# Q and K of a block's first 14 tokens, projected in eight pieces between the early steps

## Chip, cores and metric

One core of one Trainium2 chip runs the whole program in one launch. The metric is device time in microseconds; lower is better. All matrix work is bf16 with fp32 accumulation.

## The reference

Two layers share one set of weights. Each is an attention over segments with a memory that is handed from segment to segment, followed by a gated feed-forward block:

```python
def attention(x, mem0, Wq, Wk, Wv, Wo):         # x: 2048 x 512 after layernorm; 32 heads of 128
    mem = mem0                                  # 8 x 512
    for s in range(64):                         # segments of 32 tokens
        h = concat(mem, x[32*s : 32*s + 32])    # 40 x 512
        q, k, v = h @ Wq, h @ Wk, h @ Wv        # 32 heads each
        p = softmax(mask(q @ k.T / sqrt(128)))
        o = (p @ v) @ Wo                        # 40 x 512
        mem = o[:8]                             # the next segment needs it
        out.append(o[8:])

x = x + attention(layernorm(x));  x = x + (sigmoid(n @ w_gate) * (n @ w_up)) @ w_down   # n = layernorm(x)
x = x + attention(layernorm(x));  x = x + (sigmoid(n @ w_gate) * (n @ w_up)) @ w_down
```

The loop over segments is a recurrence through `mem`. The 32 tokens of a segment, though, are known as soon as the layer's input is, so Q and K of those columns can be projected at any earlier time.

## The kernel before

**Steps.** Work goes in 70 steps. Step t handles segment t of layer 1 and, since layer 2 runs `LAG` = 6 segments behind, segment t-6 of layer 2 in the same instructions. In steps 0 to 5 only layer 1 is there (40 columns: 32 tokens and 8 of memory); in steps 6 to 63 both are (80 columns). A tile `hT` of a step holds the transposed columns in the order tokens of layer 1, memory of layer 1, memory of layer 2, tokens of layer 2. Four segments make a block (`BLK` = 4); after a block's last step `ffn` does its feed-forward work, from weights that are streamed in again each time by POOL's queue.

**A step** (`emit_step`). For groups of heads: `qk` (L874) multiplies Wq and Wk of three heads with the step's columns, eight matmuls of 128 rows a head; ScalarE copies the result from PSUM into `qku`; `sc` (L910) makes the scores; VectorE and ScalarE do the softmax; TensorE transposes the probabilities (L956), multiplies them with V (L982), and ScalarE copies that for `wom` (L1001), the product with Wo, which adds up over all heads in one PSUM bank. At the end VectorE copies the memory columns of that bank into the next step's `hT`, and the next step's `qk` can begin.

**Q and K ahead, as it is.** Steps 0 to 5 (`save`) carry 14 columns more than they need: `early_x` puts the first `NE` = 14 tokens of segment t+6 beside step t's 40 columns, so their `qk` matmuls have 54. The 14 columns of the result are copied into the tile `kx` and written to DRAM (`xq`). Steps 6 to 11 (`load`) read them back into `kx` by two loads on SP's queue (L804), copy them into `qku`, and multiply only the other 66 of 80 columns. From step 12 on `qk` has all 80.

**V ahead.** V of most tokens is projected by blocks (`v_group`, `v_pass`, `v_half`; matmuls of 512 columns at L641 and L679) and parked in DRAM (`scr`); a step reads its rows back into `vsb`. The remaining rows are projected in the step (`strips`, L768). The first 80 us do much of this while the weights arrive: SP's queue loads x, then Wv, Wq, Wk and Wo in parts (L519).

**What sets the order.** All work is first recorded as tasks (`pl.add`) with an engine or a choice of two, what they read and write, and an expected duration. `plan` then takes the order of all tasks, and the choice of engine, from a table written into the kernel (`SEQUENCE`, packed text); every engine issues its tasks in that order. `warm` finds places where TensorE is expected to wait over 250 ns and puts filler there: matmuls of a constant tile `hot` into a bank that is free (L1220), in front of the task that waits.

Buffers that matter here: eight PSUM banks (of kind "v" at most three at a time), three staging tiles `vst` of 512 columns that also serve `v_pass`, one tile `kx`.

Of the kernel before, what the change touches and what calls it, by code (L numbers as in the profile page):

```python
# [53 lines left out]
;BKuiVqE|X01NF@%`%$~C5I~V(&DA-OaXtS+oZAk*3k2dJAGvJ`K4rePyr97!Bi{jAHvv%XkRPRfF1TT>3QycOz)(#e7JiZh6=G4BCJyZTa`JjKaw7+_W?k=$6E})3{EOU@GEuz+<S997ZSBsC!UPa`3e^OcZc13UF_jWS_=U@M@Vu  # L54
)?^Jk+S=(nw>o9DjP1NW3k@!Y_JvoI|uSU^QcNCqKm!gxq=`#yCwshxTDLA)Esn^P=$o2#QhSXJq(Ug3|%_wZHnr}Tl_8Z5$+bO03=t|i9?h)?`DR|SsM+Cg&Q?uJ7Bb&sM`2$8v5VHI4nX@*_zXJ05tlt4G$dGzRdZgTL<-u&a!b=
@yXD+zAM8o)rkKOOOuT%HjZRRL_{T^RPv4*|xcO5RXV=8|vZdOw~vpuIyD3^h_6_(A`=3*UfXk+MN9-~d!d-F_dazit{3lXzFn4BJDju4I$46aE|5_!KMwM-+{4PZ7=vHhEyrb&trStNg=4v!m&cAib3%XKKTArFzcQnDlVtgi=)r8
om6Tqq0hLSc931v$`+{_hxn&#7>e1&Az!rOqqPzot<B=D!hO!SyNy?EltBsrbbJpVxv~mXa;L5b~YBU_f$G4VudeQ*O3(>9AvtDlJl{OKBrhU{?6^(=*-Xgwy%hEA)pX44PC^cU^ZmHZ3MCZ*t+;jvC3A_RS$G(Mj7-m`+=WurRZCy
RW28zY7)FoKbost*~b%bZa@p9jN9cHa0Yt#Fzoq4}Ya6mu*)8mcMdw_TJ}CFun0bZMFoV`@4WV>ZR0&vP9|2gE)7d0;@^3vbJsTS)a>Nn=?8EEV1tyZdHth)Ps%K&0<+YcBg|=mAGw8Z{T$*B$OQXT?`{9_o_=h4Xf@73+l@K@Kme7
rTSsNNj$U9aapJ}H@bt|&}0{(8m6TP_0`)w1k-LLm8QCEkk}#PT!IvUZ6`Xx4Ge@-SbjIku4K}0ZoTQur#5otl1{TM^N@TVrJK05=6dxx6T!)_#&JRPWOW?D8_q?1TFdHI5+%-wf);%E?rF3!zC6aZS^<U)sHFB24*bp$eA;{k#*u^
)yy~3m94a{iSuUi?=4SqpCg0p{$w6;cQ{`lv7cW?N%fW!cuXF?7C*b-`ybmC^kr#Z-J1<heQyb3#2Up@yTPY&0g!9H6G#q^RL%goi?9>D&+~tB;9w*b9FgG^XE9=@znb2^<(RBb%VO6eSCVaTWMr;d7r2Bp7u6%+tb>K}1o1$s{136  # L60
KU8Yq|t?_cZE3@=kH4`QW0A<NzV-JkMZB(}*7%LIjmclfqBq7!$M74E!j!t*BMXqjfU+Q2CzTCdu4Fsl?_uuFc<h~6XInEz1iO2>9s2UTmG>4oe)=lAWxqM$>B0#G?Zu)+Q<t|2J1oFIwFvj;e52}KJI>ZhF1JeKj<C<UFGaLv+^-a
pAwsEME4Iv{n%6vMj{i@)b(^3eOK$-Pg!P~%9_7__A*&GXfos!9O|R`Crii%XP^iyZ;`e$f{i)WZuj46Q$$21D7gIr>`JVAJG6ah(f8_s`Lyq2H9j8exyRpWI(#2{M9LD}qZ7pc4|rdJ_8et4OQ;%}a4H^7OQO#DK&p#!rV8^saoyz
87|7bq9VZKoVb6R9I6kNICzvq9rwU>%jiouIYe%Q<u8s8#_i<uTIoT6)-~}3rs!CZs0JK!SS^PSF>Z|t%dXwaS{CX5r#c9(7FT`{Je^*W6kvuv*lyA%(tm^A|YF1Jln6_Q^?fIOWKsFDd=~{D_7cmM&1XVT4FP?8u74bXi%Xx8Lv_b
2gEgT>83KhZBh-1D5!-Knh%wDJaXAjI$p>F4#VWG`mMKZ##Wu(jLTwC_HL22@uc&Nh7<%C$mv6P@;zUwqMO_#%nq=Ya0oenG9LHcaQA+$IBLHpL_&->{@1>-)FQ3$9J>csOv>QDjyee-((A@%asEwA$#}=Muifq>i~4=p6C%msT14k
_I^w>aA2ocBy$^2F8Uy7K8n$OyPLUE3(;AtnL?z2Q5qgrLT_!w<A|b|DIddq#P>B=-$4c&4#WZEY59`AIIEgUZkBJB`y6Ow-qJw5NN?9gjbrbYKB$qUfhB0fx8yx~ZYieTn78*megD#UaIvxCc$+(}_-GlDTglIzBWa9-xNNX;7w`H
ht&Y@+sLo}%F2fS(sv%ktXl&Sz~K^|?0Skg*JY^ok%+ns~LB%q%5w%x@(ne?a8-_VqYY@+h_M^x^iF$3C^ILRBFeq+%*{z?{q$HnX27bK}z3RQE!6+t`Dig!>vOwXNma_iWBPclA;X08N<QZVz~O<B|B5I9&ZLwCs4@8gc&Y5^z}e0
l(+eqe=rU}UqzX4tyL+JK9*n;h)g)k%h>ZQkfDMqk6rA&--EcT{5ha1wTP$IhTO`oZt4OT9mcfJKv&I}!e!*ao=|OXL+wz5Ufv<uKzvsCT_X{{Ygjboh>5zWCKt3Aw}4nr28wy7D@iwKnOyWg{16OcVpIpzeIE{B`2_hCJN-g3Dv(Y
~1LYUP8yQQZAWqPCcd9+_r#5y^F$mR5RfCfX{<qM3bp*52j@@kGCY;&b&3$2ejznzF1RoFaRo!Se#yU?~e2LZJ<u^O*0;vjlczqF$=x!zRl472-RPEL1k~Al&Uxsd6|49mY{jEw^6wK+=lig6!5kJsDRk67Vh@gy6w4I48-$36E9sf
9Mnbu5I@Xd0=d3-uMUzd1nAo#A8nBnkwbq7qvOO*D#~N%zaB1-or!_ht1&0DlEr^>fYPfAqmv>4_tvFs__7$}vtBrk3MmyvCj`+}>J=4&2Vu{F$}%c#s(<aP26uBGMvP(R{_61{SscPw?48<sKKTo(kR>F&(PzG7sw@Cu#4x~^3FV3
p+RNUftl>~V^~%5LvqgQjtFQu`E^_*s`JkX={RM)F1q1>0xYLnEQ0YZQnxSc{scP+?m|WF3pUBGyYi3+D@p;}<s_#1M=%x5|i}|_*($A|TI@63`)AR|>j+?0vf%CE_nHu0seH~qWD`0;Dt}L0FDzJ+9dVF}|iN}@}4rIqQ=?f+J#qH  # L70
i5)Psi_x}I&HQ15}yl7;&_?*&9REL9(KKGF@`xtjg0WnrDb@X*T$rA2-2H78#ee|+Bn&x8w!q{9!Q+>x9oP{sQt#ekY0>*<jpmFpELF7WCfhqE$;YoSEGk61*EouQjWT9MY?W?pEvesBU{l+XHfx0KDJn*&s!hh|!iR)4a8#AiPmv1
LLvXv$dln`A*56_FAuosO*3x!tHHrtdxis{4pe_VAJv8Xi!}B9_F^{<{YosaIxAXNE#&ART>Y91Gj?n7?E3w%XVP(K%eR1a6eSh{Wc8lrJV2$2^L41fr}A#WZR$HdDxdBmsJI(O-;C)cqJ4j?e;~68CX(PvmlCxQ~8{Ua^Qi9#MB0m
4me2(-p-_#ZawJlsR90iaX|P<JHeB+#|4!P)jGgNt>=}eT;tn-PltAX+v<_!HTy<EI)#DyUxZfF>@9k^l7*^UN7PSMm+?BB_eeP;Vh~2F6bCbx&5c2<9ifiDWs01i2==!t};cEkd8K9Do}9%z*w+_Jb6a`<{<<h+e9|klTz3$R0n4m
HexQ=jm2_pHC06xDlLAcW5xKl-i9IgE2nhjw=jDVm!N@O0^;M*&L5@!Zm{&u_`2$p1Doa0NYcNaDZ0K86kXk4o5Ij9HH4;*Oj)A*SPCiv|3x%RDy2+?{6$8+$9oS;L3o4cwdy)Z--^K8D5oD0!6au3D(|Mk%x|49a@v4?00%EdS_q&
&j{SeY$?tyO-u6%Jbo3{b=(C?rZpU}wWC?2bk3;7D+<(#z(N9|oJAeovUsP=nL}sO~o^v2XGhvqSf#3ur`fg;G<oG_aP0TC8pdD;+m`%+W`FZWJr9*WuVJa4#er6%KT86U28;ae(udg<Zv-k-R@h1&QTDMk3o!vuAIJYyIirJf56?d
<-Xfwr#?i-;<41>kClzy8YfqbArK~VEII-;^6si}H~MC`i|M)0X_o~panNVgdjCDwkCp3*0Eg0gz|M*q!i)1?HxY&Jj@+6y`LG!<b{Np=6*5d#2R)#_9uM*sbRO;kOuMMvNP`(8>w6=D+r=rG~ZP&VYBeAGe;^o?2zy6^PBvEx(!6e
z$(yT{5&bxb%&f{awSd#<q~lUusQ{q^|yIgb-Ug+9yV@y0x=_Or8ki1m3q2r<hKx=$#t3s}d`hC~DThmGDnt+xBj*nI=&JmHi_cN#Z0m1L?AI(%ZuK518W$^{<j1hQdwxyz^^@Wafmd{g7v{J;aAzKTQ#GrKLoh+ygzNs5W#FJ=&uG
p}|l^?GB@`bAn6L5+g}$iK$sDY=DwkpX5YHfW{`cKOKQzSD}uDVA4`3`8ma`lL3ieNQ<{{n~T1K%_AgySyZBcLHq*S?lD?%6{JK0KH~F*m?dId|LM4e<lme1S~c!`aE6)-8EjHlvzPipQTO7f;b^<w&X};tDvuBThQQ;Oi=AW;%pU%
e?&D+1t*aW+-$`958=7mXNn=nm{UejM#e0eox1kyG<Jsd2+jt`E=D21V|sx)PXO;yKyRB)U_1Iy&X|Q?Pp}qE2Le}*HPLdcdoslscFd|r(lXC=3Wv=xOK;SBhq1)Bx>Zc<sEr+E&_(wpMhb=w%wR9vA_6DN2k`=9xkchYzG-PXJM(~
?9j$9`lwJK$&tLKsDjugE3x3*yngo^{VFMY=2UObS^~@URJ+vPKvCL7?E6L)NYLXiA-hQ}8<(%MkY0Go3SAgaTrh>jJ`2h!ebyh<YC_fd`17Se@Htq?96`@17%k4Vk?FESFz}b#+^%RkZy8(^tZy%-YWVW$_*;}crd{F@zG_3GGXqw  # L80
G$9YbO)XtO6x_2x4eAxF~Tx;YX>4Ton*ZIXOmY03|wPRSI+sWtMxKXZzfi$noh?)@d+bdqY?!!<znNBuZ7ILccEGMRc)vR0tTD0D;h2X!;aw|#g6`N&SLl9&rZM7F;Twhvx7ptEb(ySd7Yx-Y?k%UDpv#&6StRh28w(Op9D#Z9_ztV
#;M;o3gZY*0*O1@k*QgZ_@VKb%ETY<92_C84tPMi@sI*R@=&Jgl!`Y#|eF7^f%5u^aLe&$CO(^AXGpQKS8P*^^ZvWeEyyp)5C17s=UoD<v6qQSf-jI;;2@L#ook`wTvNlXl_eCj#GL;wwg;kXIkGJ@j6gY^*%KgGSAHmQu@m$_QGS;
@N3g#*u34lpDnGWe!+4XdJ!DEQc_4;RjyH=TRjZA%~v_N$M?|iz3AD-?n_6=^68K#Hzbp9T5+0AjYLm@Bx0P|7#2k2Gh(E2}w-EmJ`4~XsE#(uF>F)zN@78laFrAqHmXlcJ^bm6QLuC)|nG6&+!ZJa$#r|sI+<;fsl(d=%^g%_(iw_
;Z0Bfox{geN`_XCHr3hb@^a^d7xwpE)>1;3;$MT2c?FNa7{tKwf*_l0=23qV_VCkVRH3IXP+@V+>Y?ObbN?HPeP2eU)6U!CshZViN0Jbm0xLN7x`LGhlCKvnCfV@-EV#sWUI^$e$=Zw$+?Nve7RY^fzZoi@4j6>G{e=K{aefg<A@48
lV9kv${kUq+PQtv{yCrJ@?07o}LLmc*1y6X#Q4>ftsa6ksw#MEqE6ikW&hL<`z1;YPhm9((mxU}JF{MRi+`EW)q1dyu2S!ZLrwUX`PfwprgCc5IP2T%IjHEB|t4-lhTd+xP_nckYf<2sG`{vXqb^E)8JP7r5YUMUwcoC`k!Uj(6XCV
20LIxln5Br6W+7(5|H2wHnXwTJS-z6%PGJ(YbY#<!L3m+OpZjVvBv6k{?C9fUtev?!d!Vq_qzc2vj9o!)N*N7s9@=eje51mZhi5x04VDab1XUBgh?ohnGkI>{R+rCttLf+3VSQ)WD`gkqAsStra-r`|dY4V%#AcUMlKYJ_x_~m}mKB
h2m9rH+(T$7op<c;<;og)g_X9bb2=zEGIH|xeA(2Oz+wXT%wrv!60HlrXgBhExJ_s+hYvm{cDXwQ<Q-+2Gv;$;^SlY>ZHn^Q!*#p1d=O6$^$Ve)!Vp#-pIE;$ePR-{svt?B(Zi%!OY9pl<#`p+=kD5@Sb6(bP6@@Va1>1V|>pu!4f;
5%ea8<L^Oyr+svjR@9YJ5Kf<&<>Ar^d7p{N)UuT6skTarIdgc%>!l)%Y~GT5f|-@9G??!<Qa+x9;k0y%G|S9C%VlKV&l_1x){)sH{^$ljb=-yRIkrRQ)UMN0lyj>PGOPSn&e!sjA6jBssbpx{vx>Jqx>o^)s~cov<06%RzAOEKi~<Y
ECQ;@LI7CDY(YDT5hquVL;w~I;_SiK3kuHBwys1Wa<QwQEYISFKbf@ESgj^VG_^?qWyJ)q{_LM0#rZxpQT}|JyTU1Us1tpr))C2dQ*N=(j>U!;KWSu|!g~xms)5xiF#4BSECHxX+CFDyYbrrm(e%4*%BE|T&vEF)6?%EGmyed~A%j7
(Uz<xluJdR+&hXUd|MsBK!7)=Ohihk>MSsY>!bl91J&8t)XCtqA3@O^|M@?;8#L5&lIlmBW+Y<HIabtT_r)T&~LBA&U-p?(#d>yM_tba8Mec%9rKiWC&`CeZ{z%LSnEhyuLJt~7ysp2BR4l9U81tGX@lUbB;YA?Rz;cqlgPI59VGAd  # L90
8*Vf)3*jKqqaKi+mI%BZ-3Ekgl+vDSkZ580)w9*T`y+U2>!oBdMF3e0nfwns6&NbNylou~X_hy2vF+r2Y&OnTT;(t*@wh7~t3bSCsmgmw!erLqjuppC-YP!`&qR79#9NcJonlup=X&QuWM^6DTSZ1J^g4CP&lv&w(dvj8(Nh+|B+TN
N}GzW~xJ4ialVe$%hQqrvsuF-MGB5P;A`h{`HNxqAkn@?!CSlEFe{IKbdbXSaP~!?+l7;-^5xTlsSBtB?1Hcwu?yxzCcPB)x&8pIx)pu468wT}15Mn0Xw&Ts`;ey$?<V7<Gw3A-*xjqOQKBbrvo#0CmNQj~2$gxOO>pv%ICkMNQg$G
={ug{z-8{Jg$ZFCkIhp@H5}gg}U0$sO*zWcq0j4b|Gw~clm9{+IU7){C_y8XDm%NEv8yMkiGd0(z?YH9NgU*;TE#yo;@k5S*=IDt9XhFj@q?bzUN4)$Nh;#LXZ`XsWP)7@K84L1&M*BPx-cY7T{Fr$hTMf+=_4X?8GvmQxMI=Lbsn^
# [1206 lines left out]
```

## Time and profile before

| | us |
|---|---|
| median of 3 runs | 1747.89 |
| lowest, highest | 1745.29, 1750.98 |
| the profiled execution | 1748.87 |
| its span, first to last instruction | 1746.8 |
| TensorE busy in the span | 1733.3 |

The rows of the profile are read so: a group or timeline row names line, engine, operation, the tile written and those read, and shapes; "128x54" after the tiles is the matmul's moving operand, 54 columns. A record of a matmul lasts from its issue to its last result, so records of matmuls that follow each other overlap, and the pace is the distance of their starts. Times are from the start of the span.

### The profile page before, as it was taken

The numbers are of one execution on the slowest core, as the hardware profiler recorded it, in microseconds if no ns is written. First come the engines' busy times: TensorE is split into PE (matmuls) and PEld (weight loads), VectorE is DVE, ScalarE is ACT, GpSimd is POOL, SyncE is SP. The second block draws the span as 40 slices with busy tenths as digits, with TensorE's granted clock in tenths as the row PEclk, the third lists the DMA queues.
The fourth block names the chain that finished last, engine by engine and source line by source line (L and its number), as shares of the span: only waits on it lengthen the run. The fifth ranks groups of instructions, "written<-read, shape, count | busy, mean of one in ns | idle before, by whom it ended". The sixth has DMA issues, their size and how long they took to land.

```text
span 1746.8 us, 91799 instructions
## 1 busy us (share of the span) xinstructions
PE 1733.3 (99%) x39151; PEld 1492.4 (85%) x39151; DVE 1253.9 (72%) x4185; ACT 1143.3 (65%) x3142; POOL 873.5 (50%) x1402
## 2 busy tenths in 40 slices
PE   9999999999999999999999999999999999999998
...
PEclk9999999999999999999999999999999999999999
DMA  9835365655545464646456464646556454555544
GB/s 312 304 103 167 87 177 139 176 144 158 151 132 170 131 185 126 174 125 173 139 152 179 126 177 127 171 124 167 168 134 176 138 152 131 159 150 138 162 135 119
DMA packets 145071, 273.41 MB, mean 157 GB/s; under 512 B 39846, under 2 KB 85930, under 8 KB 144662
## 3 DMA queue, kind: packets, MB, share of 16 engines
...
HBM read 221.78 MB, written 27.07 MB: 142 GB/s over the span
## 4 chain that ended last, share of the span: by engine, by line
PE 94%; DMA 2%; issue 1%; SPq 1%; POOL 1%; ACT 0%; DVE 0%; POOLq 0%
PE bank L874 33%; PE bank L1001 17%; PE bank L1103 11%; PE bank L768 7%; PE bank L641 7%; PE bank L1126 5%; PE bank L910 4%; PE bank L982 4%; PE bank L956 2%; DMA wk_sb<-in_A_Wk_dram 1%; PE bank L601 1%; SPq L1230 1%; PE bank L1071 0%; DMA vsb<-sst 0%; DMA xs<-in_A_x_dram 0%
## 5 line engine op out<-in xcount | busy, mean ns | idle before, releaser
L874 PE MATMUL bank<-hT,wk_sb 128*128 128x80 bf16 (+3 forms) x8960 | 616.9, 198 | 2.3 <-DMA wk_sb<-in_A_Wk_dram 1.8
L874 PE MATMUL bank<-hT,wq_sb 128*128 128x80 bf16 (+3 forms) x8960 | 616.5, 198 | 0.6 <-DVE hT L1014 0.3
L1234 ACT CAST qku<-bank 128x480 bf16<-128x480 f32 (+3 forms) x770 | 383.6, 506 | 208.3 <-PE bank L874 183.7
L874 PEld LDWEIGHTS <-wq_sb 128*128 128x128 bf16 x8960 | 454.0, 99 | 31.6 <-issue 14.3
L874 PEld LDWEIGHTS <-wk_sb 128*128 128x128 bf16 x8960 | 447.5, 99 | 2.9 <-DMA wk_sb<-in_A_Wk_dram 1.9
L1001 PE MATMUL bank<-otsb,wo_sb 128*128 128x80 bf16 (+1 forms) x8960 | 356.2, 198 | 1.9 <-issue 1.9
L924 DVE TENSOR_TENSOR st<-bank,cst 40x240 f32<-40x240 f32 (+3 forms) x768 | 281.2, 368 | 101.2 <-PE bank L910 85.1
L1001 PEld LDWEIGHTS <-wo_sb 128*128 128x128 bf16 x8960 | 333.5, 99 | 12.4 <-issue 2.7
L1230 POOL DMA_DIRECT2D vsb<-sst x360 | 182.2, 510 | 185.9 <-ACT sst L1234 73.7
L1234 ACT CAST otsb<-bank 128x480 bf16<-128x480 f32 (+3 forms) x420 | 199.9, 482 | 83.0 <-PE bank L982 48.6
L1120 POOL DMA_DIRECT2D wd<-in_B_w_down_dram x217 | 156.9, 723 | 136.5 <-PE bank L1126 43.0
L1095 POOL DMA_DIRECT2D wg<-in_B_w_gate_dram x217 | 166.2, 766 | 113.3 <-PE bank L1103 54.7
L1096 POOL DMA_DIRECT2D wu<-in_B_w_up_dram x217 | 166.3, 767 | 108.1 <-PE bank L1103 34.5
L934 ACT ACTIVATE st<-st 80x240 f32<-80x240 f32 (+3 forms) x420 | 159.1, 381 | 70.2 <-DVE st L931 66.9
L1226 ACT ACTIVATE ptsb<-bank,small 80x160 bf16<-80x160 bf16 (+3 forms) x444 | 163.3, 385 | 16.4 <-PE bank L956 10.1
L1103 PE MATMUL bank<-xnT,wg 128*128 128x128 bf16 (+2 forms) x1784 | 171.4, 218 | 0.0
L1103 PE MATMUL bank<-xnT,wu 128*128 128x128 bf16 (+2 forms) x1784 | 171.0, 218 | 0.0
L936 DVE TENSOR_REDUCE small<-st 80x6 f32<-80x240 f32 (+3 forms) x420 | 151.6, 363 | 25.7 <-ACT st L934 23.6
L1230 POOL DMA_DIRECT2D vsb<-scr x197 | 104.7, 532 | 121.4 <-PE bank L982 62.0
L931 DVE TENSOR_TENSOR st<-st,small 80x240 f32<-80x240 f32 (+3 forms) x420 | 155.7, 372 | 7.7
L945 DVE TENSOR_TENSOR pb<-st,small 80x240 bf16<-80x240 f32 (+3 forms) x420 | 154.6, 371 | 7.3
L910 PE MATMUL bank<-qku 128*128 128x80 bf16 (+1 forms) x2240 | 158.6, 197 | 0.4 <-issue 0.4
(108 smaller groups left out, 2604.1 us busy)
## 6 DMA issues: line engine op xcount, KB each, us to landing
...
vsb<-scr SPq DMA_DIRECT2D x120, 66.0 KB
vsb<-scr POOLq DMA_DIRECT2D x110, 66.0 KB, 3.5
...
```

The costliest lines, as they stand in the source:

```text
L874: nc.tensor.matmul(o_ap, lhsT=W[:, c, h * P:(h + 1) * P], rhs=mv(c), start=(c == 0), stop=(c == DC - 1))
L910: nc.tensor.matmul(s_all(SB)[:, w0 + i, :], lhsT=fview(qku[:, i, 0, 0:1], [(1, P)]), rhs=qku[:, i, 1, 0:ncol], start=True, stop=True)
L924: pl.add("DVE", dve_ns(n, True), lambda gsz=gsz, hs=hs, st=st, SB=SB, pj_=pj_, npj_=npj_, mk=mk, idx=idx: nc.vector.tensor_tensor(out=st[p ...
L934: pl.add("ACT", act_ns(n), lambda hs=hs, st=st: nc.scalar.activation(out=st[pr, hs], in_=st[pr, hs], func=ACTF.Exp, scale=self.scale), r=s ...
L1001: nc.tensor.matmul(WB[:, c * ncol:(c + 1) * ncol], lhsT=self.wo[:, h, c * P:(c + 1) * P], rhs=otsb[:, hl, 0:ncol], start=(h == 0 and c == ...
L1095: pl.add("POOL", 760, lambda wg=wg, fs=fs: nc.gpsimd.dma_start(out=wg[:], in_=self.wgv[:, :, fs]), r=[("wo", self.H - 1)], w=[gk] + bt, la ...
L1096: pl.add("POOL", 760, lambda wu=wu, fs=fs: nc.gpsimd.dma_start(out=wu[:], in_=self.wuv[:, :, fs]), r=[("wo", self.H - 1)], w=[uk] + bt, la ...
L1103: nc.tensor.matmul(gu[:, 2 * i + k, 0:n], lhsT=W[:, c, i * P:(i + 1) * P], rhs=xnT[:, c, rw], start=(c == 0), stop=(c == DC - 1))
L1120: pl.add("POOL", 760, lambda wd=wd, ip=ip: nc.gpsimd.dma_start(out=wd[:], in_=self.wdv[:, 2 * ip:2 * ip + 2, :]), w=[dk] + (["boot"] if se ...
L1226: nc.scalar.activation(out=dst, in_=src, func=ACTF.Copy, scale=by)
L1230: {"SP": nc.sync, "POOL": nc.gpsimd}[tk.on].dma_start(out=got[1], in_=got[2])
L1234: nc.scalar.copy(out=dst, in_=src)
```

## The change

The first 14 tokens of the four segments of steps 12 to 15 (block 3 of layer 1) get the same treatment, but no step carries them. When block 3 is normalised for its V, the 4 x 14 columns are also copied into a new tile `xe`. A new function `early_qk` makes eight pieces from it, one for each four heads: 32 matmuls of 56 columns into one bank, one copy into a staging tile, one write to new rows of `xq`. The tasks are recorded before step 0; where they run is in the table. Steps 12 to 15 become `load` steps: two loads each into `kx`, copies into `qku`, 66 columns in `qk`.

`SEQUENCE` is new as well. The orders of the two built programs are the same on TensorE from shortly before step 21 on, and differ before that, the weight loads of the first 80 us among the rest.

```diff
-;BKuiVqE|X01NF@
...
+;BQSY@Ld1_fBiGK
...
-        self.xq = dr.tile([self.LAG * P, H * 2 * NE], BF16, name="xq")
+        self.xq = dr.tile([(self.LAG + BLK) * P, H * 2 * NE], BF16, name="xq")
+        self.xe = c.tile([P, DC, BLK * NE], BF16, name="xe")
...
+            if b * BLK == 2 * self.LAG:
+                dst = fview(self.xe[:, 0, 0:1], [(BLK * NE, self.DC), (NE, BLK), (1, NE)])
+                self.pl.add(("ACT", "DVE"), copy_ns(4 * BLK * NE, True), lambda pst=pst, dst=dst: (dst, fview(pst()[:, 0, 0:1], [(P, self.DC), (SEG, BLK), (1, NE)])), r=[B], w=["xe"])
...
+    def early_qk(self):
+
+        nc, pl, DC, w = self.nc, self.pl, self.DC, BLK * NE
+        rows = self.xq[self.LAG * P:(self.LAG + BLK) * P, :].rearrange("(i p) e -> p i e", p=P)
+        for k in range(self.H // 4):
+            B = pl.buf(self.bank, "v")
+            vs = pl.buf(self.vstp)
+
+            def mm(k=k, B=B):
+                for i in range(4):
+                    for m, W in ((0, self.wq), (1, self.wk)):
+                        for c in range(DC):
+                            nc.tensor.matmul(B[:, (2 * i + m) * w:(2 * i + m + 1) * w], lhsT=W[:, c, (4 * k + i) * P:(4 * k + i + 1) * P], rhs=self.xe[:, c, :],
+                                             start=(c == 0), stop=(c == DC - 1))
+
+            pl.add("PE", 8 * DC * mm_ns(w), mm, r=["xe"] + [(n, h) for h in range(4 * k, 4 * k + 4) for n in ("wq", "wk")], w=[B], use=[vs])
+            pl.add(("ACT", "DVE"), copy_ns(8 * w), lambda vs=vs, B=B: (fview(vs[:, 0:1], [(NE, 8), (8 * NE, BLK), (1, NE)]), B[:, 0:8 * w].rearrange("p (a i n) -> p a i n", a=8, i=BLK)),
+                   r=[B], w=[(vs, 0)], use=[vs])
+            pl.add("SP", 700, lambda vs=vs, k=k: nc.sync.dma_start(out=rows[:, :, 8 * NE * k:8 * NE * (k + 1)], in_=vs[:, 0:8 * w].rearrange("p (i e) -> p i e", i=BLK)),
+                   r=[(vs, 0)], w=[("xqb", k)], lat=3000.0, use=[vs], nb=P * 8 * w * 2)
...
-        save, load = t < LAG, LAG <= t < 2 * LAG
+        save, load = t < LAG, LAG <= t < 2 * LAG + BLK
...
-                       r=[("xq", t - LAG, lo)], w=[("kx", p) for p in range(lo, hi)], lat=3500.0, nb=P * (hi - lo) * w * 2)
+                       r=[("xq", t - LAG, lo)] if t < 2 * LAG else [("xqb", k) for k in range(lo // 4, hi // 4)], w=[("kx", p) for p in range(lo, hi)], lat=3500.0, nb=P * (hi - lo) * w * 2)
...
         self.v_group([8, 10, 11, 13], {}, cuts, 2)
+        self.early_qk()
```

More of the change, by code (lines that the diff above doesn't have):

```diff
@@ L57 @@
[L57 to L60, printed above, removed]
@@ L139 @@
[L139 to L141 removed]
+;BQSY@Ld1_fBiGK4}q&Kti%91_Mt;v?h1iQFD%IJk=5MNAZP67X|5E5Dp`LCR8F(bTwe&l2UYb^CtHa-I!^>HO(37uyG~JcL+=^VF=>&KG8OB-d|<cR{#)itJ2O?s#ejD}^@gh&R;dPo1e9o>kq;P>|L!etvk{dXvp4pfXvM-%fQO^
```

172 lines of the change are left out of this document (88 added, 84 removed).

## The prediction

> **What bounds the kernel now.** I read the page first, then the chain of waits, then a table of windows cut at the starts of the steps, then the timeline of TensorE around those cuts.
>
> ```profile
> span 1746.8 us, 91799 instructions
> ...
> PE 1733.3 (99%) x39151; PEld 1492.4 (85%) x39151; DVE 1253.9 (72%) x4185; ACT 1143.3 (65%) x3142; POOL 873.5 (50%) x1402
> ...
> PE   9999999999999999999999999999999999999998
> ...
> PEclk9999999999999999999999999999999999999999
> DMA  9835365655545464646456464646556454555544
> ```
>
> TensorE has hardly a free slice at full clock; DMA is full only in the first slice or two. So time is the sum of TensorE's paces plus the places where it waits or runs filler, and a change is worth what it does to that sum. The start is different: the chain of waits between 30 and 100 us shows where the DMA hands over to TensorE.
>
> ```profile
> 40.62 3.28 SPq L1230
> 43.95 10.57 DMA wk_sb<-in_A_Wk_dram
> 54.56 2.16 PE bank L874 x44
> ```
>
> SP's queue stands 3.28 us at a small transfer (L1230), issues a load of wk at 43.95, and TensorE is held for it until 54.56. From there to the end the chain is TensorE's. The steps begin (first matmul of L874 of each) at 40.4, 78.7, 95.7, 112.3, 128.8, 148.2, 171.1, 194.5, 214.7; steps 9 to 11 end at 311.6 and steps 12 to 15 at 410.2, so the windows below are steps 1 to 7, then 8 to 11, then 12 to 15.
>
> ```profile
> 78.70:95.70 17.00, 16.76 (x495) 13.85 (x494) 13.67 (x46) 11.74 (x45) 7.31 (x13) 1.00 0.39 110
> 95.70:112.30 16.60, 16.60 (x496) 13.77 (x495) 13.29 (x49) 12.29 (x46) 5.28 (x10) 1.00 0.41 113
> 112.30:128.80 16.50, 16.41 (x499) 14.03 (x498) 12.89 (x48) 12.47 (x48) 7.20 (x12) 1.00 0.38 106
> 128.80:148.20 19.40, 19.40 (x562) 17.25 (x561) 14.37 (x53) 13.92 (x50) 9.38 (x14) 1.00 0.53 151
> 148.20:171.10 22.90, 22.22 (x579) 17.62 (x578) 15.63 (x53) 14.47 (x54) 9.58 (x14) 1.00 0.62 180
> 171.10:194.50 23.40, 23.21 (x510) 18.66 (x509) 16.93 (x60) 16.78 (x48) 8.29 (x15) 1.00 0.45 120
> 194.50:214.70 20.20, 19.79 (x492) 16.89 (x491) 13.47 (x51) 16.60 (x50) 4.57 (x9) 1.00 0.25 64
> 214.70:311.60 96.90, 96.86 (x2268) 84.07 (x2267) 73.69 (x257) 70.24 (x209) 53.09 (x85) 1.00 0.57 160
> 311.60:410.20 98.60, 98.60 (x2204) 87.91 (x2201) 73.05 (x246) 65.46 (x169) 50.24 (x79) 1.00 0.54 153
> ```
>
> Columns: length, then busy time of PE, PEld, DVE, ACT, POOL. In steps 1 to 7 TensorE is idle 1.61 us in all (the differences of the first two numbers). In steps 8 to 15 it is idle 0.04 us of 195.5. The same windows for the filler alone (L1220, matmuls on a constant tile that keep TensorE going where the plan expects a wait) end in this sum:
>
> ```profile
> sum 136.00, PE 3.84 PEld 1.07; mean PE 0.55 PEld 0.15
> ```
>
> So early steps hold 3.84 us of work that computes nothing (3.4 by start to next start, since a record's tail overlaps the next matmul). This is the room that the change can use.
>
> **The change part by part.** Paces come from starts in the timeline (start, length, what):
>
> ```profile
> 94.49 0.96 PE L1001 MATMUL bank<-otsb,wo_sb 128*128 128x40 bf16 x32
> 95.30 0.48 PE L1220 MATMUL bank<-hot 128*128 128x512 bf16 x2
> 95.73 0.26 PE L874 MATMUL bank<-hT,wq_sb 128*128 128x54 bf16 x4
> ...
> 96.03 0.26 PE L874 MATMUL bank<-hT,wk_sb 128*128 128x54 bf16 x4
> ...
> 96.84 0.26 PE L874 MATMUL bank<-hT,wk_sb 128*128 128x54 bf16 x4
> ```
>
> ```profile
> 214.25 0.39 PE L601 MATMUL bank<-cst,xn 128*128 128x128 bf16 x4
> 214.74 0.28 PE L874 MATMUL bank<-hT,wq_sb 128*128 128x66 bf16 x4
> ...
> 215.46 0.39 PE L1071 MATMUL bank<-cst,oxT 128*128 128x128 bf16 x4
> ```
>
> ```profile
> 315.90 0.31 PE L874 MATMUL bank<-hT,wq_sb 128*128 128x80 bf16 x4
> ...
> 316.75 0.27 PE L910 MATMUL bank<-qku 128*128 128x80 bf16 x3
> ```
>
> 54 columns: 32 matmuls in 0.81 us, 25.3 ns each. 66 columns: 24 in 0.72 us, 30.0 ns. 80 columns: 24 in 0.85 us, 35.4 ns.
>
> *Removed.* Steps 12 to 15 make 256 Q and K matmuls each, now of 66 columns instead of 80: 1024 x 5.4 ns = 5.5 us. That stretch is TensorE throughout, so all of it counts.
>
> *Added on TensorE.* Eight pieces of 32 matmuls with 56 columns. No row has 56; between 25.3 (54) and 30.0 (66) it is 25.3 to 26.1, so 256 x 25.7 = 6.6 us. By itself the trade therefore loses 1.1 us. The Trainium skill's page "TensorE: Matmul & The Clock Gate", section "Part 1: The HAM clock gate", speaks against the change in the same way: N/2.4 GHz plus some 2.5 ns for each matmul, never under about 25 ns. By its figures the estimate would be 6.0 us saved against 6.6 spent, a loss of 0.6 in place of 1.1; the rows are used here.
>
> *Where the pieces stand.* In the built program's order every filler matmul after step 0 and up to step 8 is gone (15 of them) and the pieces stand at the end of step 2, in and after step 3, in step 4, in and after step 5, and two in the tail of step 7. In the old order the fillers stood at the ends of steps 1 and 2, in step 4, after step 5 and (six) in step 7. V matmuls of each step from 1 on are the same in number up to step 16, and the two orders are equal from step 21 on. So the pieces take the place of filler and of waits. A step's tail is a chain: last Wo matmul, copy of the memory columns, first Q and K of the next step. The row pair 94.49/95.73 prices it: 32 matmuls at 25 ns end at 95.3, the next step starts at 95.73, so 0.43 us, which one piece (0.82 us) covers and exceeds.
>
> *What the pieces displace.* Filler: 3.4 us. Waits: at least 0, as a wait may begin only after the piece; at most 4.2 us, which is what all starts of steps 1 to 7 lie behind their paces. Of that 1.61 is the idle time above; the rest is hidden, as each record lasts some 0.2 us past its pace. The larger ones (over 0.1 us) are 17. The first and the longest, from the chain and from the list of TensorE's waits:
>
> ```profile
> 87.69 0.24 issue
> ```
>
> ```profile
> PE bank L1126 <- DMA wd<-in_B_w_down_dram: 0.6, 1, 0.6
> ```
>
> The last is in the rows above: four transposes from 214.25 end their pace at about 214.5 and the next step begins at 214.74. I go by places: piece for filler at the ends of steps 2 and 5 and in step 4 +0.9, the two pieces of step 3 +1.3, the first of step 5 +0.5 (a DMA wait of 0.6 stands near), step 7's pair 0.2 less 0.6 of its waits, step 1's filler against a shorter wait -0.2: together +2.1 us, that is 1.1 us of waits covered. Range -1.0 (6.6-3.4-4.2) to +3.2 (none covered).
>
> *Start.* Up to step 1 the work is the same 192 V matmuls, in another order, and SP's loads come in another order. Counted from that order, 13.85 MB stand on SP's queue up to the wk load that held TensorE at 54.56; its counterpart now (the pair of wk loads of six heads) ends at 14.24 MB. At 13.85 MB in 54.56 us, 0.25 MB/us, that is 1.5 us later. V matmuls have this row:
>
> ```profile
> 26.99 7.07 PE L641 MATMUL bank<-wv_sb,xvf 128*128 128x512 bf16 x32
> ```
>
> That is 0.22 us each. Behind the hold, up to step 1, the old order has 64 V matmuls of 512 columns and 132 of Q and K, the new one 60 and 108: 4 x 0.22 + 24 x 0.025, with a few small ones some 1.7 us less. So it cancels: 0, range -1 to +3, the upper end from a second hold (below).
>
> *ScalarE, VectorE, SP.*
>
> ```profile
> L1234 ACT CAST qku<-bank 128x480 bf16<-128x480 f32 x520 | 285.5, 557 | 160.2 <-PE bank L874 146.3 <-PE bank L956 4.8 <-PE bank L910 2.6
> ...
> L1234 ACT CAST qku<-bank 128x396 bf16<-128x396 f32 x60 | 28.9, 488 | 10.7 <-PE bank L874 9.4 <-PE bank L956 0.8
> ...
> L1234 ACT COPY qku<-kx 128x84 bf16<-128x84 bf16 x39 | 9.5, 262 | 1.2 <-PE bank L910 1.1
> ```
>
> Steps 12 to 15 gain 44 copies from kx at 262 ns on ScalarE (11.5 us if all go there, fewer on VectorE) and save 44 x 69 ns = 3.0 us: +8.5 us in 98.6 us where ScalarE is busy 65.5. Steps 8 to 11 already run so, ScalarE at 70.2 of 96.9 and TensorE without idle time, and ScalarE's qku copies wait for TensorE, not the reverse. Hence nothing. The eight eviction copies (448 columns, between 488 and 557 ns) are 4.2 us spread over steps 3 to 8, where ScalarE has some 4 us or more free in each. If that cover is missing, a score matmul waits up to 0.5 us per piece, inside the range. SP gets 8 writes and 8 loads more; behind a piece's write, which waits for its copy, stand the V reads of the next step, and their attention matmuls (L982) would wait for them. DMA is under 0.7 there, so I take nothing.
>
> Sum: -5.5 + 2.1 + 0 = -3.4 us. The profiled execution took 1748.87 (2.1 around its span), 1.0 over the median of 1747.89 and within the runs' 1745.3 to 1751.0. So 1745.5 for it and 1744.5 for the median.
>
> **The rivals.**
>
> *A, all waits covered.* Pieces cost -1.0, the start gains its 1: -7.5, 1740.4. For it: the waits' number (17) and the pieces' places in the same tails. Against: 0.6 us of them is a DMA wait for wd and the pieces are 0.82 us long where tails are 0.43.
>
> *B, the start, ending slower.*
>
> ```profile
> 52.46 0.28 PE L874 MATMUL bank<-hT,wq_sb 128*128 128x54 bf16 x4
> 54.56 0.36 PE L874 MATMUL bank<-hT,wk_sb 128*128 128x54 bf16 x4 [1.83 <-DMA wk_sb<-in_A_Wk_dram]
> 54.75 0.36 PE L874 MATMUL bank<-hT,wq_sb 128*128 128x54 bf16 x4
> 54.93 0.36 PE L874 MATMUL bank<-hT,wk_sb 128*128 128x54 bf16 x4
> ```
>
> ```profile
> 40.00:60.00 20.00, 17.39 (x257) 10.37 (x254) 8.33 (x23) 6.97 (x19) 14.66 (x28) 0.91 0.99 352
> ```
>
> The hold of 1.83 us is followed by matmuls at 0.18 us for four, 45 ns instead of 25.3, and the granted clock of the window, 0.91 (the third number from the end), means some 3.6 of its 20 us at half speed. The 44 matmuls of the chain's row lost 0.9 us by it, the whole at most 1.8; I take 1.4. The new order starts Q and K some 4 us earlier and then wants the wq load of heads 9 to 15, 9.79 MB into SP's queue: 38.6 us at the rate above. TensorE arrives at 40.4 less 12 V matmuls and plus 48 of Q and K, 39.0, with no slack. If SP's queue stands at a small transfer as it did for 3.28 us, this is a hold of 3.3 with 1.4 of half clock, and the later one grows by as much: up to +7 us, and -3.4 + 7 = +3.6, 1751.5. It decides from a loss of 3.4 us at the start on. Against: a first hold is swallowed when a later load binds anyway. The Trainium skill's page "TensorE: Matmul & The Clock Gate", section "Part 1: The HAM clock gate", has the clock fall after an idle window of about 3.4 us; by that a hold of 1.83 would cost no half clock, which this trace contradicts with its 45 ns.
>
> *C, the pieces do not do what they are for.* Filler goes, but the waits under it come back as idle time next to the pieces: 6.6 - 5.5 = +1.1, 1749.0. For it: steps 2 and 5 put a piece at a tail of 0.43 us, longer than the wait. Against: a tail cannot wait while a piece runs.
>
> **How the numbers follow.** The forecast has 0.55 (its own range -6.5 to -0.5: 1741.4 to 1747.4), A 0.2, B 0.15, C 0.1. Predicted time 1744.5. Range 1740.4 (A) to 1749.5, past C and into B; what B gives beyond is left out with part of A, under 2 in 10. 0.3% is 5.2 us, about what a measurement of this kernel can tell from no change: under 1742.6 lie A and a tenth of the forecast, 0.25; over 1753.1 the far end of B, 0.08; between, 0.67.
>
> **What would show it.** Steps 12 to 15 should take 93.1 us and show 30 ns per Q and K matmul; steps 1 to 7 some 138 us with no L1220 at all; step 1 should begin at 78.7 within some 2 us. Wrong would be: step 1 beginning after 82 (B), steps 1 to 7 under 136 (A), idle time of TensorE over 3 us in them (C), or waits for kx or qku in steps 12 to 15, which I cost at nothing.

## The result, and the profile after

In the first comparison the changed kernel took 1751.57 us (median of 20 runs, 1747.89 to 1754.7) against 1747.19 for the kernel before (20 runs, 1743.2 to 1750.98): ratio 1.0024, 95% interval 1.0017 to 1.0032. Three later comparisons, each on a chip of its own, gave 1.0009 (1.0000 to 1.0017), 1.0010 (1.0002 to 1.0019) and 1.0011 (1.0003 to 1.0020). So it is slower, by 0.7 to 1.8 us there (one of the intervals begins at 1.0000) and by 4.4 us in the first comparison; 1744.5 us and a gain of 3.4 had been forecast.

From the page of the changed kernel (its profiled execution took 1752.87 us):

```profile
span 1751.2 us, 92167 instructions
...
PE 1718.1 (98%) x39177; PEld 1490.9 (85%) x39391; DVE 1250.8 (71%) x4178; ACT 1151.9 (66%) x3202; POOL 868.9 (50%) x1395
...
q8 instruction: 309, 5.06, 1.2%
...
PE 89%; DMA 4%; DVE 3%; issue 1%; SPq 1%; ACT 0%; POOL 0%; DVEq 0%; POOLq 0%; ACTq 0%
```

This trace lacks 214 records of matmuls (39177 against 39391 weight loads), so TensorE's busy time reads too low; starts of steps are the safe measure. DMA has 4% of the chain of waits, where it had 2%. The same stretches as before the change (steps 1 to 7 one by one, 8 to 11, 12 to 15):

```profile
79.50:97.40 17.90, 16.91 (x500) 14.12 (x500) 12.60 (x46) 12.53 (x44) 5.69 (x10) 1.00 0.43 119
97.40:114.40 17.00, 16.92 (x524) 14.34 (x525) 14.03 (x52) 12.44 (x45) 4.75 (x8) 1.00 0.42 116
114.40:132.00 17.60, 17.33 (x560) 15.21 (x558) 12.56 (x44) 13.16 (x51) 5.23 (x9) 1.00 0.41 112
132.00:151.70 19.70, 19.54 (x595) 17.87 (x595) 15.31 (x54) 13.32 (x49) 7.78 (x12) 1.00 0.54 142
151.70:175.90 24.20, 23.05 (x638) 19.16 (x641) 16.04 (x55) 16.54 (x60) 12.84 (x20) 1.00 0.72 205
175.90:199.10 23.20, 22.94 (x507) 18.50 (x511) 15.66 (x54) 17.52 (x49) 7.85 (x15) 1.00 0.37 98
199.10:219.00 19.90, 19.57 (x551) 18.05 (x550) 13.65 (x52) 17.10 (x54) 7.62 (x16) 1.00 0.27 74
219.00:316.10 97.10, 96.30 (x2255) 84.09 (x2269) 72.31 (x252) 71.32 (x215) 51.78 (x83) 1.00 0.59 163
316.10:410.00 93.90, 92.44 (x2190) 82.24 (x2201) 72.50 (x248) 68.38 (x206) 49.43 (x77) 1.00 0.61 171
```

Steps 12 to 15 went from 98.6 to 93.9, as wanted. Steps 1 to 7 went from 136.0 to 139.5. Step 16 begins at 410.0 where it began at 410.2, so up to there the change is level, and in this pair of profiles 4.6 us are lost behind it, where the orders of work are the same. That was the surprise, and the experiments start from it.

The loss behind step 16 consists of single gaps in TensorE's work with no other engine behind them. One from the timeline:

```profile
1698.73 0.25 PE L900 MATMUL bank<-hT,wk_sb 128*128 128x40 bf16 x4
1698.83 0.18 PE L900 MATMUL bank<-hT,wq_sb 128*128 128x40 bf16 x1
1700.25 0.24 PE L900 MATMUL bank<-hT,wq_sb 128*128 128x40 bf16 x3 [1.24 <-issue]
```

TensorE stops behind the first of four matmuls that add into the same place and read the same tiles: the other three have nothing to wait for. In the 1.00 us before, the DMA queue of instructions moves one packet, which keeps one of 16 engines busy for 0.93 us (5.8%):

```profile
q8 instruction: 1, 0.02, 5.8%
```

The trace has 39391 weight loads, to each of which a matmul belongs, and 383 waiting instructions, 79165 TensorE instructions in all, and the page counts 309 packets of 16 KB: 256 instructions in each. Counted so, ten such gaps of over 0.3 us in this trace and six in that of the kernel before stand at instruction 194 or 195 of 256, and each ends 1.3 to 1.6 us after such a packet has landed. So they are waits for the instruction fetch ("fetch stalls" below). The change adds 482 instructions, and so shifts all later work by 226 of 256 against these breaks.

### The profile page after: what moved, and what is told of

It reads as the page before. It is cut to its first block, busy times and chain, and to the rows that moved or that the text cites. A ratio compares the mean times of both kernels' runs of the same rounds, so it can differ in the third digit from the quotient of the medians.

```text
span 1751.2 us, 92167 instructions
## 1 busy us (share of the span) xinstructions
PE 1718.1 (98%) x39177; PEld 1490.9 (85%) x39391; DVE 1250.8 (71%) x4178; ACT 1151.9 (66%) x3202; POOL 868.9 (50%) x1395
## 4 chain that ended last, share of the span: by engine, by line
PE 89%; DMA 4%; DVE 3%; issue 1%; SPq 1%; ACT 0%; POOL 0%; DVEq 0%; POOLq 0%; ACTq 0%
PE bank L900 31%; PE bank L1027 17%; PE bank L1129 11%; PE bank L794 7%; PE bank L643 6%; PE bank L1008 4%; PE bank L936 4%; PE bank L1152 4%; PE bank L982 2%; DMA wo_sb<-in_A_Wo_dram 1%; DMA wq_sb<-in_A_Wq_dram 1%; PE bank L603 1%; DVE st L950 1%; DMA vsb<-sst 1%; DMA scr<-vst 1%
## 5 line engine op out<-in xcount | busy, mean ns | idle before, releaser
L900 PE MATMUL bank<-hT,wq_sb 128*128 128x80 bf16 (+3 forms) x8960 | 610.3, 197 | 3.8 <-issue 1.2
L900 PE MATMUL bank<-hT,wk_sb 128*128 128x80 bf16 (+3 forms) x8960 | 610.6, 197 | 2.2 <-issue 2.2
L1261 ACT CAST qku<-bank 128x480 bf16<-128x480 f32 (+4 forms) x770 | 380.1, 502 | 189.5 <-PE bank L900 161.7
L950 DVE TENSOR_TENSOR st<-bank,cst 40x240 f32<-40x240 f32 (+3 forms) x768 | 281.1, 369 | 115.0 <-PE bank L936 98.7
L1253 ACT ACTIVATE ptsb<-bank,small 80x160 bf16<-80x160 bf16 (+4 forms) x440 | 161.8, 385 | 17.0 <-PE bank L982 11.6
```

The lines of the kernel that those rows point to most:

```text
L900: nc.tensor.matmul(o_ap, lhsT=W[:, c, h * P:(h + 1) * P], rhs=mv(c), start=(c == 0), stop=(c == DC - 1))
L950: pl.add("DVE", dve_ns(n, True), lambda gsz=gsz, hs=hs, st=st, SB=SB, pj_=pj_, npj_=npj_, mk=mk, idx=idx: nc.vector.tensor_tensor(out=st[p ...
L1253: nc.scalar.activation(out=dst, in_=src, func=ACTF.Copy, scale=by)
L1261: nc.scalar.copy(out=dst, in_=src)
```

## The experiments

The table holds what all of them rest on: the length of each stretch by the starts of the steps (first matmul of `qk`), and the fetch stalls of the whole profile in sum (gaps at the breaks of over 60 ns that end 1.2 to 1.7 us after the landing, less the usual 35 ns). The last stretch ends with the end of the last matmul.

| profile | step 1 begins | 1 to 7 | 8 to 11 | 12 to 15 | 16 to 67 | 68 and 69 | fetch stalls |
|---|---|---|---|---|---|---|---|
| before, first | 78.7 | 136.1 | 96.9 | 98.6 | 1285.0 | 48.3 | 5.0 |
| before, again | 78.2 | 135.4 | 96.9 | 98.6 | 1283.0 | 46.9 | 2.1 |
| before with xe | 76.0 | 135.1 | 96.9 | 98.6 | 1284.1 | 46.7 | 2.7 |
| before, no filler | 78.4 | 135.8 | 97.0 | 98.6 | 1284.1 | 48.2 | 5.1 |
| the same again | 78.9 | 135.0 | 96.9 | 98.6 | 1283.2 | 47.6 | 3.5 |
| no filler, 15 in step 0 | 77.6 | 135.7 | 96.9 | 98.7 | 1283.5 | 46.7 | 3.7 |
| changed, first | 79.5 | 139.5 | 97.1 | 94.0 | 1287.8 | 50.1 | 10.1 |
| changed, second | 77.8 | 140.0 | 97.3 | 93.4 | 1284.2 | 47.5 | 5.5 |
| changed, third | 79.1 | 138.8 | 97.6 | 93.3 | 1283.9 | 48.1 | 5.0 |
| changed, fourth | 80.4 | 138.9 | 97.3 | 93.7 | 1283.8 | 47.3 | 3.2 |
| changed, xe moved | 79.3 | 139.9 | 97.4 | 93.3 | 1283.7 | 48.1 | 5.1 |
| 15 matmuls at piece | 79.9 | 138.2 | 97.1 | 93.5 | 1283.6 | 47.0 | 3.3 |
| 15 in step 0 | 79.2 | 139.3 | 97.1 | 93.2 | 1284.8 | 47.0 | 4.6 |
| the same again | 77.7 | 138.1 | 97.1 | 93.7 | 1284.1 | 46.7 | 2.9 |
| half pieces | 78.5 | 137.4 | 97.3 | 93.1 | 1284.1 | 47.7 | 4.7 |
| double pieces | 78.9 | 144.8 | 97.1 | 93.1 | 1287.8 | 47.1 | 6.2 |
| 80 columns | 79.5 | 138.2 | 97.3 | 98.6 | 1284.8 | 48.0 | 4.8 |

**Again, for a second profile of each.**

> The changed kernel once more, unaltered, for a second profile. In the first profiles the change is ahead by 0.2 us when step 16 begins and loses 4.6 us behind it, where the orders of work are equal. Theory F (instruction fetch): TensorE's instructions come 256 at a time, the breaks lie at instruction 194 of each 256, and the change moves all later work by 482 instructions (226 of 256) against them; then the same places stall again (steps 32, 51, 62, 68 and 69) and the time is again 4 us above the kernel before. Theory J (jitter): the late stalls fall elsewhere in every execution, the second profile's late part differs from the kernel before by less than 1.5 us either way, and the 4.4 us come from the early steps, which this profile must then show.

> The kernel before once more, unaltered: both theories expect 1747 us and a ratio of 1.000. Its profile shows how far two profiles of one kernel differ by place. F: late stalls at the same work as in the first profile of it (1661, 1682, 1703, 1724 and 1729 us) and none of over 0.5 us at 813 to 842 us. J: they move.

Measured: 1746.06 us, ratio 1.0009, and 1745.92, ratio 1.0002 (0.9993 to 1.0010), beside 1745.34. The late stalls moved in both kernels: step 32, which had lost 1.8 us, lost 0.2, and the last two steps took 47.5 for 50.1. The first pair of profiles had shown chance together with the effect. Not all was chance: between 420 and 1640 us the changed kernel again had a fetch stall (0.4 us at 496 us), the kernel before again none.

**The place against the breaks, restored in the changed kernel.**

```diff
             def mm(k=k, B=B):
+                for _ in range(15 if k == 0 else 0):
+                    nc.tensor.matmul(B[:, 0:w], lhsT=self.wq[:, 0, 0:P], rhs=self.xe[:, 0, :], start=True, stop=True)
```

> The changed kernel with 15 more matmuls of 56 columns ahead of the first piece, whose result is overwritten: 30 TensorE instructions, so that all work behind it stands against the breaks of the instruction fetch as it does in the kernel before. F: the late part is that of the kernel before, 4.6 us are won back and 0.4 us (15 x 25.7 ns) paid, 1747.4 us. J, or a cause in where tiles lie: 0.4 us slower than the changed kernel, 1752.0 us.

Measured: 1744.66 us, ratio 1.0000 (0.9991 to 1.0008), 1.4 us under the changed kernel on the same chip although it does more. Later the 15 matmuls were made one column wide and put among the fillers of step 0 (`made` counts these):

```diff
+                    for _ in range(15 if made == 21 else 0):
+                        nc.tensor.matmul(B[:, 0:1], lhsT=self.hot[:], rhs=self.hot[:, 0:1], start=True, stop=True)
```

> The changed kernel with 15 matmuls of one column more among the fillers of step 0, where TensorE waits for its first data: 30 instructions at no cost in time, so that all later work stands against the breaks of the instruction fetch as in the kernel before. F: 2 us less than the changed kernel (the run with 15 matmuls at the first piece was 1.4 us less and had paid 0.4), level with the kernel before. A and J: as the changed kernel, ratio 1.001.

> The changed kernel a fourth time, unaltered, beside the next three. Theory F (the place of the later work against the breaks of the instruction fetch costs 1 to 1.5 us): ratio 1.001, and fetch stalls between 420 and 1640 us of 0.4 us or more in all, as in seven of the eight profiles so far that have this place (0.4 to 3.4 us; the kernel before without its fillers had 0.04). Theory J (chance): level with the run with the place restored, fetch stalls there anywhere from 0 on.

> The changed kernel with the 15 one-column matmuls in step 0 again. F: 1 to 1.5 us under the run beside it without them, no fetch stall over 0.2 us between 420 and 1640 us, as in all five profiles so far that have the place of the kernel before. J: no difference.

Measured: 1745.13 us, ratio 1.0002 (0.9993 to 1.0011); then, side by side, 1746.30 unaltered (1.0011) and 1745.91 with the 15 (1.0004, 0.9995 to 1.0012). Every time the median is lower with the place restored, by 1.4, 1.5 (against the run with xe moved, below, which differs in more than the place) and 0.4 us. Single intervals overlap, so the size is uncertain. The profiles say the same: fetch stalls between 420 and 1640 us add up to 0.4 us or more in all eight profiles of the changed kernel and its variants with its place, and to 0.2, 0.0 and 0.0 us in the three with the place restored. From step 16 to the end they are 2.8 to 8.4 us in those eight and 1.9 to 2.5 in these three.

**The same place given to the kernel before.** Its 15 fillers of steps 1 to 8 are 30 instructions, so leaving them out gives the changed kernel's place:

```diff
                     B, n = fill[tk.idx]
+                    made += -(-n // 4)
+                    if 22 < made <= 37:
+                        n = 0
```

> The kernel before without the 15 filler matmuls of steps 1 to 8, nothing else: 30 TensorE instructions less, so that all work behind them stands against the breaks of the instruction fetch as it does in the changed kernel. F: the late part is that of the changed kernel, 4.6 us slower from step 16 on, less what the filler cost (0 to 3.4 us): 1748.4 to 1751.8 us. J or tile places: nothing late, 1743.8 us if the filler only delayed, 1747.2 us if the waits under it come back.

> The kernel before without the 15 fillers again: its later work has the changed kernel's place, and yet it was 0.5 to 1.1 us under the kernel before. F: fetch stalls of 0.4 us or more between 420 and 1640 us and 1 us over the next run, which shares all but the place. J: level with the next run.

> The kernel before without the 15 fillers, with 15 one-column matmuls in step 0 instead, so that its later work has the place of the kernel before. F: 1 us under the run without them, fetch stalls between 420 and 1640 us under 0.2 us. J: level with it, and both within 0.5 us of the kernel before, since the waits under the fillers came back.

Measured: 1744.27 us, ratio 0.9996 (0.9988 to 1.0005); again 1744.52, 0.9999; with 15 one-column matmuls in step 0 on top 1744.41, 0.9999. Here the place costs nothing that shows, and no fetch stall over 0.05 us stands between 420 and 1640 us. So the place by itself isn't the cause; as far as these medians can tell it costs only together with something else in the changed kernel, and what that is stays open.

These runs settle another thing: filler is worth nothing. Without it steps 1 to 7 take 135.0 to 135.8 us, as with it, and the list of TensorE's waits in them (run again, steps 1 to 7) shows what stood under it:

```profile
PE bank L874 <- DVE hT L1019: 0.6, 2, 0.3
PE bank L874 <- issue: 0.5, 1, 0.5
PE bank L956 <- DVE pb L945: 0.5, 1, 0.5
PE bank L1126 <- DMA wd<-in_B_w_down_dram: 0.4, 1, 0.4
PE bank L768 <- DVE hT L1239: 0.4, 1, 0.4
PE bank L1001 <- ACT otsb L1237: 0.4, 1, 0.4
```

**The price of the pieces.**

```diff
-                        for c in range(DC):
+                        for c in range(DC // 2):
...
-                                             start=(c == 0), stop=(c == DC - 1))
+                                             start=(c == 0), stop=(c == DC // 2 - 1))
```

> The changed kernel with half of each piece's matmuls (two of four parts of the sum are left out, so the first 14 columns of Q and K in steps 12 to 15 are wrong): 128 matmuls or 256 instructions less, so that the later work keeps its place against the breaks of the instruction fetch. Theory P (every piece matmul costs its pace): 3.3 us less than the changed kernel, all in steps 2 to 7. Theory W (they cover waits, as the forecast had it): 2.2 us less or under, since the waits come back. Theory F (the early steps are limited by the instruction fetch, some 4.2 to 5 us per 128 matmuls): 4.2 to 5.0 us less.

```diff
-                for i in range(4):
+                for i in (0, 1, 2, 3, 0, 1, 2, 3):
```

> The changed kernel with each piece's matmuls made twice (the second time over the first): 256 matmuls or 512 instructions more, the later work keeps its place against the breaks of the instruction fetch. P and W (nothing is left to cover): 6.6 us more than the changed kernel, all in steps 2 to 7. F: 8.4 to 10 us more.

> The changed kernel a third time, unaltered, beside the next three. It was 4.4 us above the kernel before in the first comparison and 0.7 us in the second. Theory S (the loss is in the early steps): steps 1 to 7 take 139 to 140 us against 135.5 to 136 before, steps 12 to 15 93.4 to 93.9 against 98.6, step 16 begins level with the kernel before or up to 1.5 us early, and what is left of the difference is chance of the late stalls: ratio 1.000 to 1.001. Theory L (the change makes the late part slower by itself): from step 16 to the end 1335 us or more, against 1330 to 1333.5 in the kernel before; ratio 1.002.

Measured on one chip: 1747.55 us unaltered (ratio 1.0010), 1745.03 with half (2.5 less), 1753.40 with double (5.9 more). The windows of steps 1 to 7, half, unaltered and double:

```profile
78.50:215.90 137.40, 133.38 (x3727) 114.19 (x3741) 99.58 (x354) 102.69 (x350) 51.73 (x88) 1.00 0.46 128
```

```profile
79.05:217.81 138.76, 136.20 (x3855) 117.20 (x3869) 99.81 (x354) 102.82 (x350) 51.77 (x88) 1.00 0.46 127
```

```profile
78.90:223.70 144.80, 143.03 (x4111) 123.77 (x4125) 100.20 (x354) 103.35 (x350) 51.80 (x88) 1.00 0.43 122
```

From none (135.5, the mean without filler or pieces) the first 128 matmuls cost 1.9 us, the next 128 cost 1.4, 256 more cost 6.0. At 25.7 ns they would be 3.3, 3.3 and 6.6. So the pieces do cover waits, and beyond them little is left to cover. How much they cover can't be read from these lengths alone: they also hold waits for late V rows (0.8 us with half, 0.9 unaltered, none with double), and the four profiles of the unaltered kernel lie between 138.8 and 140.0. The limit by the fetch (4.2 us or more for 128 matmuls) is refuted as a steady pace.

**The saving.**

```diff
+        skip = NE if load and t >= 2 * LAG else 0
...
-            return hT[:, c, q0:q1]
+            return hT[:, c, q0 - skip:q1]
...
```

> The changed kernel with all 80 columns multiplied again in steps 12 to 15 (the pieces are made and used as before, the first 14 columns of these matmuls are not read): the saving alone is undone. By the forecast's paces 1024 x 5.4 ns: 5.5 us more than the changed kernel. By the first two pairs of profiles (98.6 against 93.4 to 93.9 us) 5.0 us more, since stalls at the load of kx or the score matmuls take a part. If ScalarE's copies from kx delay that stretch, it stays above 98.6 us.

Measured: 1751.21 us, 3.7 over the unaltered one by medians, ratio 1.0042 (1.0025 to 1.0058) to the kernel before. Its window of steps 12 to 15, and that of the unaltered kernel on that chip:

```profile
315.00:413.60 98.60, 97.86 (x2191) 88.00 (x2202) 73.53 (x248) 68.83 (x206) 49.48 (x77) 1.00 0.57 164
```

```profile
315.45:408.79 93.34, 92.43 (x2190) 82.31 (x2201) 72.39 (x248) 68.36 (x206) 49.45 (x77) 1.00 0.61 173
```

5.3 us in this stretch, and every other stretch differs by less than 1 us in these two profiles; with 80 columns it is back at 98.6 even with the copies from `kx`.

**Where the tiles lie.**

```diff
+        self.xe = c.tile([P, DC, BLK * NE], BF16, name="xe")
         self.hff = [c.tile([P, FC, P], BF16, name=f"hff{i}") for i in range(1)]
```

> The kernel before with the tile xe allocated where the change allocates it and never used: 448 bytes that move hff, the V inputs and the tiles of wg, wu and wd, nothing else. On one chip the large packets of POOL's queue (wg, wu, wd) took 222 ns in the changed kernel and 219 to 220 in the kernel before between 420 and 1640 us. Theory A (addresses): packets 222 ns here too, and with longer transfers the late stalls grow: 2 us slower, ratio 1.001 or more. Theory F (place against the breaks of the instruction fetch) and theory J (chance of single profiles): ratio 1.000, packets 219 to 220 ns.

In the other one `xe` and a tile `xr` for the pieces' rows are made last:

```diff
-        self.xq = dr.tile([(self.LAG + BLK) * P, H * 2 * NE], BF16, name="xq")
-        self.xe = c.tile([P, DC, BLK * NE], BF16, name="xe")
+        self.xq = dr.tile([self.LAG * P, H * 2 * NE], BF16, name="xq")
...
+        self.xe = c.tile([P, DC, BLK * NE], BF16, name="xe")
+        self.xr = dr.tile([BLK * P, H * 2 * NE], BF16, name="xr")
...
```

> The changed kernel with xe allocated behind all other tiles and the pieces' rows in a DRAM tile of their own, so that every other tile on the chip lies where it lies in the kernel before. A: packets 219 to 220 ns, 2 us less than the changed kernel, level with the kernel before or up to 1 us faster. F and J: as the changed kernel, ratio 1.001, packets 222 ns whatever the addresses.

Measured: 1745.06 us, ratio 0.9999 (0.9990 to 1.0008), packets 225.7 ns; and 1746.68, ratio 1.0005 (0.9996 to 1.0014), packets 223.4 ns (mean of the 4096-byte packets of POOL's queue between 420 and 1640 us; the expectations' figures are of a count that reads some 3 ns lower). The addresses do lengthen the transfers, by 1%, and it costs no time that shows.

## Why the prediction was wrong, by its own steps

The forecast was -3.4 us; by the means of the profiles the sum is +2.7. The two terms that were worked out from paces held. What failed are terms that were set at nothing or left out: in steps 1 to 7 the wait for V rows ("I take nothing"), in the start the load of Wo (0), and behind step 16 the fetch stalls, which the sum does not have and which make up the whole loss in the profiles of the first comparison.

*Removed, -5.5.* Nearly right: steps 12 to 15 fell by 4.6 to 5.3, and no wait for `kx` or `qku` over 0.3 us stands there. In the first and the fourth profile an attention matmul waits 0.5 and 0.6 us for `vsb` in step 12, which is a part of what lacks. ScalarE's added copies cost nothing, as said, and the evictions of the pieces took 543 ns each, within the 488 to 557 given.

*Added, 6.6.* Right by pace. Two groups of a piece (8 matmuls in 0.21 us, 26 ns each):

```profile
113.57 0.27 PE L746 MATMUL bank<-xe,wq_sb 128*128 128x56 bf16 x4
113.67 0.27 PE L746 MATMUL bank<-xe,wk_sb 128*128 128x56 bf16 x4
113.78 0.26 PE L746 MATMUL bank<-xe,wq_sb 128*128 128x56 bf16 x4
```

*What the pieces displace, -4.5 (filler 3.4 and waits 1.1).* Steps 1 to 7 grew by 3.8 us (139.3 against 135.5, means of the four profiles of the changed kernel and of the first three in the table), not 2.1. The filler was counted as work that goes away and the waits as something in addition; but the runs without filler take the same 135 to 136 us, so filler only fills waits, and taking it out gains nothing by itself. What a piece wins is the wait that it covers. The waits that stood under the filler (the list above) are gone from the list of the changed kernel. For the same steps the whole list of its second profile is

```profile
PE bank L1008 <- DMA vsb<-sst: 1.0, 1, 1.0
PE bank L794 <- issue: 0.9, 1, 0.9
PE bank L643 <- issue: 0.2, 1, 0.2
```

So rival C's mechanism, the return of those waits beside the pieces, did not happen; other waits came. Step by step, by the same means, steps 2, 3, 4 and 7, which hold six of the eight pieces, grew by 1.4 us, and the forecast's places give 1.5 for them (its 0.9 for three places split evenly). Steps 1, 5 and 6 grew by 2.4 us where the forecast has 0.6, though steps 1 and 6 hold no piece.

*V rows, "I take nothing".* This is the step that failed in steps 1 to 7: a wait that the forecast named and priced at nothing, an attention matmul waiting for `vsb`. From step 6 of the fourth profile, first TensorE's row, then SP's queue:

```profile
191.74 0.53 PE L1008 MATMUL bank<-ptsb,vsb 120*128 120x120 bf16 x7 [1.57 <-DMA vsb<-sst]
```

```profile
178.32 8.15 SPq L1257 DMA_DIRECT2D scr<-vst  x9
186.57 1.56 SPq L1257 DMA_DIRECT2D vsb<-sst  x2
```

In the kernel before the same place has

```profile
186.96 0.53 PE L982 MATMUL bank<-ptsb,vsb 120*128 120x120 bf16 x7 [0.19 <-DMA vsb<-sst]
```

In the unaltered profiles the wait was 0.9 to 1.6 us in sum over steps 1 to 7 (in the first in step 1, in the second and fourth in step 6, in the third in both), against 0 to 0.3 before; on average 0.9 more. In step 6 it is not a piece's write that stands ahead of the V rows on SP's queue, as the forecast had thought, but nine writes of earlier V rows, where the kernel before has eight. By the semaphore updates in these traces the last of a late load's 16 parts lands 1.4 to 2.2 us behind the other fifteen. That the new order, and not chance of the transfers, makes them late was not tried by itself. Fetch stalls in the same steps came to 1.3 us against 0.8 before. Two profiles have no wait for V rows in these steps, "15 matmuls at piece" and "80 columns": they grew by 2.7 us each, of which 0.4 in the first is its 15 matmuls, near the forecast's 2.1. No run has the new order without the pieces, so what the order costs by itself is not separated.

*Start, 0 (-1 to +3).* In the range, at its upper half: step 1 begins at 79.2 against 77.6 (the same means; all profiles with the one or the other start and nothing added to it give 1.2 us between them). A part of the scatter is the clock: the 44 matmuls behind the hold for wk took 2.16 us in the first two profiles of the kernel before, at half clock as rival B read it, and 1.28 us in the third, where the granted clock stayed full. The hold did not stay with wk. In the chain of waits of the changed kernel the DMA leads until 75.84:

```profile
65.95 9.89 DMA wo_sb<-in_A_Wo_dram
75.84 0.05 issue
75.89 0.77 PE bank L1027 x24
```

and TensorE's list of waits has

```profile
PE bank L1027 <- DMA wo_sb<-in_A_Wo_dram: 2.3, 1, 2.3
```

Wo, which nothing had waited for, is now the load that ends last; in the other three unaltered profiles TensorE waits 0.7 to 2.3 us for it. A hold for wq, as rival B expected, came too, 1.1 us in the second profile and 2.7 in the third, but step 1 began no later there (77.8 and 79.1, against 79.5 and 80.4 in the first and the fourth). The forecast asked only where the two wk loads stand; it should have gone through the queue to the last load that step 0 needs.

*The later part, 0.* The step that isn't in the sum at all. Means from step 16 on: +1.8 us (1333.1 against 1331.4). Fetch stalls of the whole run: 6.0 against 3.3, most of the difference behind step 16. Taken off, both kernels' spans are 1739.9 us on average, so of the forecast's -3.4 the early steps and the start took it to 0, and the fetch stalls turned that into a loss. In the first comparison, where the changed kernel lost 4.4 us, its profile shows 10.1 us of fetch stalls against 5.0 in the kernel before, more than the whole loss, and the large packets took 228 ns in the kernel before and 230 in the changed one, later 221 to 227; that slower transfers are why it lost more there was not tested. Why the changed kernel has more of these stalls stays open: its place against the breaks has a part in it, but the same place cost the kernel before nothing.

Sum by the means: start +1.6, steps 1 to 7 +3.8, 8 to 11 +0.5 (not looked into), 12 to 15 -5.0, later +1.8, together +2.7, less 0.4 around the span (1.7 for 2.1): +2.3, between the 0.7 to 1.8 of three comparisons and the 4.4 of the first. The difference stayed inside the 0.3% that were named as the limit, on the other side of zero. Rival B named the start as the cause of a loss; it gave 1.6 of the 7 us that it could have.
